# Longer first loads, narrower modulation products, fillers around c's turning, and a new engine order in a one-core transformer block

## The chip, the core and the metric

The kernel runs on one core of a Trainium2 chip. The core has five engines that run their own instruction streams and meet only at semaphores: TensorE (PE in the profile, with its weight loads shown as PEld), VectorE (DVE), ScalarE (ACT), GpSimd (POOL) and SyncE (SP), which only issues transfers. ScalarE issues transfers too. All transfers are carried by 16 DMA engines. The metric is the device time of one execution in microseconds (us), lower is better.

## The reference

The input `x` has 2048 rows of 448 columns. Two blocks follow each other, both conditioned on a vector `c`:

```
mod = (silu(c) @ w_mod), cut in six rows: sa, ca, ga, sb, cb, gb
h = layernorm(x) * (1 + ca) + sa
q, k, v = h @ wqkv, 16 heads of 28; causal attention over a window of 256
x = x + ga * (attention @ wo)
h = layernorm(x) * (1 + cb) + sb
z = gelu(h @ w_in);  z1 = z[:, :896];  z2 = layernorm(z[:, 896:])
g = w_sp @ z2 + b_sp                      (w_sp is 2048 x 2048)
x = x + gb * ((z1 * g) @ w_out)
```

Everything is bf16 in memory. The first modulation rows, sa and ca, are needed before any query or key can be made, so `c`, the first two rows' share of `w_mod`, and the q and k columns of `wqkv` are the first things that the kernel loads beside `x`.

## The kernel before

The rows of `x` are cut in 16 tiles of 128; four tiles make a block (`tb` 0 to 3), and the 448 columns are contracted in four chunks of 112 partitions. The work has four stages that overlap at their borders.

**Front.** Loads of `x` tiles 0 and 1, of `c`, of `w_mod` (tile `wmodA`) and of the q and k weights (tile `wq_st`) are issued from SP and ScalarE in turn. TensorE turns `c` into a column with four one-column products (L514), ScalarE applies silu and writes `sc_sb` (L517), and TensorE multiplies it with `wmodA` in 32 products (L544, `t_mA`), in four groups of eight, one per load. VectorE writes the result to `modT` (L573, L574). In the meantime `x` is normalised (statistics L626 and L629, reciprocal root on GpSimd L631 and L633, application L644 or L651), transposed by TensorE for block 0 (L740), and scaled by `modT` into `hT` (L749, L751). The weights are copied from `wq_st` into a padded tile `WQK` (L615, L616, eight copies). Then K (L821), Q (L797) and V (L841) of the first tiles are made. Products of a tile of ones, called fillers (L563, 36 of them), run on TensorE where it would have nothing to do.

**Attention.** Blocks 1 to 3 are transposed by DMA (L467) and scaled on any of three engines (L730, L732). For each of 16 tiles: scores (L926, L956, L967), exponentials on ScalarE (L912), masks on VectorE (L975, L996), products with V (L1003), reciprocal and scaling (L1017, L1019), turning by DMA, the output projection (L1029), the sum (L1033) and the second norm.

**z.** TensorE makes z2 and z1 (L1123, L1144), ScalarE applies gelu.

**Mixing.** 448 products with `w_sp` (L1168), 119 with `w_out` (L1187), and the stores.

**The order is written out.** `PLAN` is a string of words such as `p42.1` or `d108`. The letter names the engine (p TensorE, a ScalarE, d VectorE, t GpSimd, s SP), the number is the operation in the order in which the code creates it, and numbers behind dots choose a PSUM bank or buffer. Every engine runs its own words in the order of the string, and it waits at each for what the operation depends on; nothing behind a waiting word can pass it. Many operations can stand on two or three engines (helpers `free`, `either`, `lock_free`), so the letter is also the choice of engine. The string was searched by a planner that is not in the kernel. The numbers that calls such as `load4` and `pe` carry (landing times, durations) and the `after` lists served that planner; the program made from a given string does not use them, other than the dependencies.

Names that the steps use: `t_x0` (loads of x tiles 0 and 1, then 2 and 3), `t_wmA`, `t_wk` and `t_wq` (first loads, two by two on SP and ScalarE), `t_cT`, `t_sc`, `t_mA`, `t_modA`, `warm` (fillers), `wqk` (copies to `WQK`). The group of q, k and v products of the tiles is made in the loop over `tb` from L700 on.

Of the kernel before, what the change touches and what calls it, by code (L numbers as in the profile page):

```python
# [17 lines left out]
p145.6 p146 a147 p136.1 p137 a138 s11 p151.5 p152 a153 p79.2 t120 t121 d123.0 d122.1 p130.7 p133.0 a134 d41  # L18
d131 t184 t185 d186.3 p68.0 p372.0 a373.2 p142.6 p143 a144 d132 d135 p154.7 p170.1 p171 p155 p378.0 s13 d241
d247 d245 s14 d308 d242 d156 d246 s15 s193 t187 t188.1 s194 p163.0 p164 t189 t190.2 s195 t191 t192.0 s196  # L20
a379.4 p397.0 t34 t35 d248 t36 d243 d382 d312 d306 d380 d309 d374 d376 p173.6 a172 p157.1 p158 p160.7 p174
a398.1 a165 p90.0 p91 d92 a399 p404.0 d402 d310 d244 d400 d169 p161 p93.0 t85 t84 a175 a159 p86.1 p87 d88 d89
p375.0 p377 p94 a405.3 a406 p425.0 p381 p383 a197 d199 t200 d198 p210.1 p211 t249 t250 t252 t253.2 t254 d95
p217.0 p218 s16 s19 a426.0.0 p433.0 d384 d385.1 p401.0 s386 a166 d407 p403 p408 a212 p204.1 p205 d311 d219
p201.0 p202 d409 s259 t255.1 d307 d313 t314 d167 d168 s260 d251.0 t256 s258 t257.3 s261 t315 t321 t319 t99 t98
t96 t97 a434.2 p453.0 d429 d203 d436 a206 p207.1 p208 p410 d411 d209 d430 d412.2 s413 d435 a162 p427.0 p220.0
p221 a454.1.1 p461.0 p229.1 p230 d457 a428 a222 p226.0 p227 d228 p431.0 p432 a462.6 p481.0 d463 a231 a482.4.2
s852 s17 s18 p437 p438 d439 d215 d440.1 s441 p223.0 p224 a225 p232.1 d458 d216 d213 d464 p489.0 a490.2 d492
p233 p235.0 p236 a237 p459.0 p455.0 p508.0 p414.0 p415 d416 t262 t264 t263 t265 a234 p387.1 p388 d389 d486
a456 p460 p465 p466 d467 d468.0 d485 t320.1 s325 t322.2 s469 s326 s21 a214 p483.0 p272.0 p273 a509.0.0 p536.0  # L30
p269.1 p270 d491 p487.0 a484 p510.0 p488 p493 a537.5.1 p516.0 d274 d316.0 s323 t317 t318.3 p494 d390 d391 t392
t393 d512 d513 d495 d496.1 s497 d394.1 t395 s324 t330 t327 t329 a271 a511 p266.1 p267 p538.0 p275.0 p276
a517.6 d519 d518 d417 p564.0 a268 p442.1 a277 p282.0 p443 p514.0 d444 d281 p515 p283 a565.4.2 d569 p544.0 d418
d445 t419 d278 p291.1 p520 p521 d522 d446 d540 d447 d541 a539 p292 a284 p288.0 p289 t448 t449 s396 t450.0 t328
t451 s20 s848 d523.1 s524 a545.2 p572.0 d546 d547 d568 a293 p294.1 p295 a290 p238.0 p239 p542.0 p543 p548
# [217 lines left out]
def bass_adaLN_cond__sliding_block__mixer_gmlp__prompt_kernel(  # L253
# [13 lines left out]
    S, D, H, DH = 2048, 448, 16, 28  # L267
# [151 lines left out]
    for row in (t_x0[:1] + t_wmA[::2] + t_wk[:1] + t_x0[1:] + t_wq[:1], [t_c] + t_wmA[1::2] + t_wk[1:] + t_wq[1:]):  # L419
        for first, then in zip(row, row[1:]):  # L420
            then.after = [first]
# [147 lines left out]
    for op in fillers[30:]:  # L569
        op.deps.update(t_mA)  # L570
# [699 lines left out]
```

## Time and profile before

| | |
|---|---|
| three timed runs | 277.41, 279.69, 281.07 us; median 279.69 |
| the profiled execution, first to last instruction (span) | 276.2 us |
| distance of the median and of the fastest run from that span | 3.5 us and 1.2 us |
| TensorE busy | 269.2 us, 97% of the span |
| VectorE, ScalarE, GpSimd busy | 164.2, 124.1, 132.6 us |
| moved by DMA | 25.55 MB |

The span runs from the first to the last instruction of one profiled execution. The time of that execution as the runs are timed is not given apart; the three runs bound what lies around the span. A busy engine is one that has an instruction in flight. For TensorE that is not the same as running at full rate: the same product can follow its predecessor after a shorter or a longer time, and this is read from the start and the length of groups in the timeline. In rows of the timeline and of the chain the first number is the start in us from the span's start, the second the length in us.

### The profile page before, as it was taken

To read this page: it belongs to the slowest core of one execution; us is meant where nothing else is said; L and a number is where in the kernel's file an instruction comes from. 1 tells how busy PE (TensorE), PEld (TensorE's weight loads), DVE (VectorE), ACT (ScalarE), POOL (GpSimd) and SP (SyncE) were. 2 spreads that over 40 slices of the span, in tenths; PEclk is the share of its full clock that TensorE was granted. 3 is DMA by queue.
4 is the path that set the end of the run, shared out by engine and by line. 5 is a ranking of instruction groups with operands and counts; after the bars stand their busy time and mean duration, and the time that the engine had idled before them with its cause. 6 is when DMAs were issued, how large, how long until landed. Compare 5 with 4: busy or idle time off the path is not lost.

```text
span 276.2 us, 8438 instructions
## 1 busy us (share of the span) xinstructions
PE 269.2 (97%) x3751; PEld 155.0 (56%) x3751; DVE 164.2 (59%) x365; ACT 124.1 (45%) x146; POOL 132.6 (48%) x190
## 2 busy tenths in 40 slices
PE   7999999999999999999999999999999999999995
PEld 5976676687667766454444444444444444445452
DVE  3698999999998999968979310014302213121454
ACT  3399999998889888365885500000000000000000
POOL 7573899629185283667567003316643303241400
PEclk9999999999999999999999999999999999999999
DMA  7999548478152586768599996000000001000114
GB/s 197 267 299 188 88 80 194 89 84 133 41 60 42 44 136 148 127 115 134 108 172 188 152 220 118 0 1 0 2 0 0 17 2 33 0 0 2 33 50 133
DMA packets 67302, 25.55 MB, mean 92 GB/s; under 512 B 58497, under 2 KB 66178, under 8 KB 67266
## 3 DMA queue, kind: packets, MB, share of 16 engines
q1 hardware_dynamic: 66304, 24.21, 47.4%
q10 hardware_dynamic: 962, 0.80, 1.2%
q8 instruction: 29, 0.48, 0.8%
q14 instruction: 7, 0.06, 0.1%
HBM read 9.01 MB, written 1.84 MB: 39 GB/s over the span
## 4 chain that ended last, share of the span: by engine, by line
PE 83%; ACT 5%; DVE 4%; DMA 4%; POOL 2%; issue 1%; SPq 0%; DVEq 0%; POOLq 0%
PE ps L1168 35%; PE ps L1123 8%; PE ps L1144 8%; PE ps L1187 8%; PE ps L956 6%; PE ps L1003 5%; ACT PW L912 5%; PE ps L1029 4%; PE ps L763 4%; PE ps L821 3%; DMA hT<-xn 2%; PE ps L841 2%; DMA wmodA<-in_w_mod_dram 2%; DVE PT L975 1%; PE ps L544 1%; DVE st_all L626 1%
## 5 line engine op out<-in xcount | busy, mean ns | idle before, releaser
L1175 POOL TENSOR_TENSOR z1T<-tmpg,z1T 128x512 bf16<-128x512 bf16 x28 | 32.1, 1153 | 75.3 <-DVE tmpg L1172 75.3
L912 ACT ACTIVATE PW<-ps 128x2048 bf16<-128x2048 f32 (+1 forms) x42 | 59.8, 1450 | 7.5 <-PE ps L956 7.0
L1172 DVE TENSOR_TENSOR tmpg<-ps,bsp_bc 128x512 bf16<-128x512 f32 x28 | 19.0, 689 | 72.9 <-PE ps L1168 68.1
L1168 PE MATMUL ps<-wspB,z 128*128 128x512 bf16 x224 | 49.3, 379 | 0.0
L1168 PE MATMUL ps<-wspA,z 128*128 128x512 bf16 x224 | 49.0, 379 | 0.0
L975 DVE TENSOR_TENSOR PT<-PW,mask 128x1024 bf16<-128x1024 bf16 x56 | 41.6, 770 | 0.3
L1168 PEld LDWEIGHTS ps<-wspA,z 128*128 128x128 bf16 x224 | 21.9, 98 | 26.5 <-issue 0.4
L1168 PEld LDWEIGHTS ps<-wspB,z 128*128 128x128 bf16 x224 | 21.9, 98 | 26.3
L633 POOL TENSOR_TENSOR rs_all<-ve_all,neghalf 128x1 f32<-128x1 f32 (+2 forms) x37 | 25.1, 691 | 14.5 <-DVE ve_all L631 8.7
L1003 PE MATMUL ps<-Vaug,PT 128*128 128x32 bf16 x496 | 23.7, 177 | 0.3 <-issue 0.3
L1003 PEld LDWEIGHTS ps<-Vaug,PT 128*128 128x128 bf16 x496 | 21.5, 96 | 2.7 <-issue 0.8
L1123 PE MATMUL ps<-w_in,hT 64*128 64x448 bf16 x224 | 22.2, 349 | 0.1
L1144 PE MATMUL ps<-hT,w_in 64*128 64x512 bf16 x196 | 22.2, 376 | 0.0
L1187 PE MATMUL ps<-w_out_g,z1T 128*128 128x448 bf16 (+2 forms) x119 | 22.0, 342 | 0.0
L1197 DVE TENSOR_TENSOR fin<-ps,x_sb 128x448 bf16<-128x448 f32 (+2 forms) x17 | 9.7, 594 | 18.5 <-PE ps L1187 17.0
L626 DVE BATCH_NORM_STATS2 st_all<-x_sb 128x6 f32<-128x448 bf16 x32 | 18.9, 613 | 2.3 <-DMA x_sb<-in_A_x_dram 2.2
L1003 PE MATMUL ps<-Vaug,PW 128*128 128x32 bf16 x224 | 20.1, 176 | 0.0
L626 DVE BATCH_NORM_STATS2 st_all<-z 128x6 f32<-128x448 bf16 x32 | 18.7, 608 | 1.8 <-ACT z L1130 1.8
L651 POOL TENSOR_SCALAR xn<-x_sb,rs_all,ve_all 128x448 bf16<-128x448 bf16 x20 | 17.1, 858 | 4.8 <-DMA hT<-xn 3.5
L1152 ACT ACTIVATE z1T<-ps 128x512 bf16<-128x512 f32 x28 | 14.7, 601 | 9.2 <-PE ps L1144 9.1
L956 PEld LDWEIGHTS ps<-qT,KT 32*128 32x128 bf16 (+1 forms) x1344 | 13.5, 90 | 8.9 <-ACT PW L912 6.4
L1003 PEld LDWEIGHTS ps<-Vaug,PW 128*128 128x128 bf16 x224 | 17.6, 96 | 1.3
(103 smaller groups left out, 369.4 us busy)
## 6 DMA issues: line engine op xcount, KB each, us to landing
out_dram<-fin SPq DMA_DIRECT2D x15, 112.0 KB, 1.7
wmodB<-in_w_mod_dram SPq DMA_DIRECT2D x1, 1568.0 KB, 14.5
x_sb<-in_A_x_dram SPq DMA_DIRECT2D x3, 448.0 KB, 9.9
w_in<-in_B_w_in_dram SPq DMA_DIRECT2D x3, 448.0 KB, 5.9
w_out_g<-in_B_w_out_dram SPq DMA_DIRECT2D x1, 784.0 KB, 5.0
bsp_bc<-in_B_b_sp_dram SPq DMA_DIRECT2D x1, 512.0 KB, 5.7
x_sb<-in_A_x_dram SPq DMA_DIRECT2D x2, 224.0 KB, 4.9
hT<-xn SPq DMA_TRANSPOSE x28, 3.6
```

The source lines that it names most:

```text
L626: st = [dve(0.62 if True else 0, lambda e, t=t, ci=ci, s=s: e.bn_stats(st_all[:, slot, t, ci, :], s()), deps(t), prio) for ci, s in enumer ...
L633: return pool(0.4 + 0.15 * len(tiles), lambda e: e.tensor_tensor(rs_all[:, slot, a:b], ve_all[:, slot, a:b], neghalf[:, 0:b - a], ALU.pow) ...
L912: ex = act(xdur, lambda e, out_ap=out_ap, in_ap=in_ap: e.activation(out_ap(), in_ap(), ACT.Exp, scale=SCALE), [s] + list(after), v - 8.0 + ...
L956: fm.append(lambda e, hm=hm, qi=qi, key=key, kn=kn, lo=lo, hi=hi, col=col, p0=p0, t=t, j=j: e.matmul(ps[p0:p0 + kn, hm.slot[t], col:col + ...
L975: return lock_d(0.68, lambda e: e.tensor_tensor(cols(hp.slot[0] * 2048 + 1024 * k, [[256, 4], [128, 2], [1, 128]]), cols(at_w() + pad + at ...
L1003: fns.append(lambda e, hp=hp, hO=hO, hi=hi, bi=bi, kb=kb, hd=hd, nb=nb, a=at[hi][bi], p_of=p_of: e.matmul(ps[:, hO.slot[0], 32 * hd:32 * h ...
L1123: return lambda e, kc, p0, start, stop: e.matmul(ps[:, hs[t % 2].slot[hf], 0:D], lhsT=hT[p0:p0 + 64, kc, t * 128:(t + 1) * 128], rhs=w_in[ ...
L1144: return lambda e, kc, p0, start, stop: e.matmul(ps[:, hs[b // 2].slot[b % 2], :], lhsT=w_in[p0:p0 + 64, kc, ft * 128:(ft + 1) * 128], rhs ...
L1168: m = pe(16 * MMS, [lambda e, h=h, si=si, ft=ft, tb=tb: e.matmul(ps[:, h.slot[0], :], lhsT=z2[:, si, ft * 128:(ft + 1) * 128], rhs=(wspA i ...
L1172: a = dve(0.7, lambda e, h=h, ht=ht, tb=tb: e.tensor_tensor(tmpg[:, ht.slot[0], :], ps[:, h.slot[0], :], bsp_bc[:, tb * 512:(tb + 1) * 512 ...
L1175: u = pool(1.16, lambda e, ht=ht, ft=ft, tb=tb: e.tensor_tensor(z1T[tb][:, ft, :], tmpg[:, ht.slot[0], :], z1T[tb][:, ft, :], ALU.mult), [ ...
L1187: return [lambda e, ft=ft: e.matmul(ps[:, h.slot[0], 0:hi - lo], lhsT=z1T[t // 4][:, ft, (t % 4) * 128:(t % 4 + 1) * 128], rhs=w_out_g[:, ...
```

## The change

- The four loads of `wmodA` and the four of `wq_st` become two each. One load brings two of the four chunks with both halves side by side, so each row that a transfer copies has 1,792 bytes in place of 896. ScalarE issues the first two chunks, SP the last two. The bytes are the same. The eight copies to `WQK` now wait by chunk pair and not by q or k.
- The 32 products of `t_mA` have a moving side of 64 columns in place of 112, and their four groups go by chunk pair first.
- `t_cT` has a filler in front of each of its four one-column products, and holds a PSUM bank for them.
- 23 fillers in place of 36: eight ahead of `t_cT`, nine between it and `t_mA`, six behind.
- `PLAN` is another string. Operation numbers are lower by 4 from the loads on and lower by 17 behind the fillers, so `p139` of before is `p122` of after. The letters change too: 365 words of VectorE become 386, 186 of GpSimd become 161, 148 of ScalarE become 150 (two of its loads are gone), 398 of TensorE become 385 (13 fillers are gone).

```diff
-d24 d22 p50.3 p52.1 p55.0 p46.1 p57.0 p54.3 a0 a3 d23 p37.0 p71.0 p63.3 p69.1 p73.0 p74.1 p61.0 p62.3 p60.2 s1
-s2 d108 d110 s4 s6 s10 s8 s12 a5 a7 a9 a38 a39 p75.1 t27 t28 t29 t32 t33 t30 t31 a100 a106 d111 d109 t112 t113
-t26 p42.1 p43 p58.3 p48.1 p44.0 p45 d114.3 d115.1 p124.6 p77.2 p64.0 p51.3 d83 p127.0 p70.1 p66.0 p72.2 p67.3
-p65.0 p78.1 d82 d125 d128 t101 p139.1 t25 t102 p56.0 d126 p81.3 p76.1 p47.0 p80.3 p59.2 p53.1 p49.2 a105 t103
-d129 p140 a141 a40 p148.5 p149 a150 d116 d118 d117 d119 d176 d180 d182 d178 d177 d183 d181 d179 t104 t107
...
+d20 a0 s1 a2 t23 s3 d19 p42.0 s5 d91 p43.0 p44.0 p45.0 s6 p46.0 p47.0 p48.0 p49.0 p33.0.0 a4 a34 s8 d18 a35
+d93 t24 t25 t28 d94 d92 p50.0 p51.0 p52.0 t29 p53.0 t26 t27 d95 t96 d98.0 p54.0 p55.0 t21 t30 a88 t32 p56.0
+p57.0 p58.0 p38.0 p39.1 p40 p41 d97.1 p107.2 t83 d66 p110.3 d65 a111 a112 t84 p59.2 p60.2 p61.2 s7 d87 d108
+d109 d90 d89 d99 d101 d100 d102 d165 d159 d161 d163 d166 t103 a86 d160 p122.2 d162 p62.2 p63.2 p64.2 a85
+p119.3 p120 t104 d164 p123 p131.0 a121 a124 p132 d106.0 p355.0 d105.1 a133 p128.1 p129 d130 a356.0 t167 t168
...
-    t_wmA = [x for v in range(2) for x in load4("d_wmA%d" % v, wmodA, w_mod, slice(v * D, v * D + D), slice(v * D, v * D + D), -98.95, ((5.4, 4.9), (6.6, 6.3))[v])]
-    t_wk = load4("d_wk", wq_st, A_wqkv, slice(D, 2 * D), slice(D, 2 * D), -98.9, (8.4, 7.9))
-    t_wq = load4("d_wq", wq_st, A_wqkv, slice(0, D), slice(0, D), -98.8, (10.4, 9.3))
-    t_x0.append(load_x0(1, "sp", -98.85, 9.6))
+    t_wmA = load4("d_wmA", wmodA, w_mod, slice(0, 2 * D), slice(0, 2 * D), -98.95, (5.0, 5.5), ("act", "sp"))
+    t_wqk_st = load4("d_wqk", wq_st, A_wqkv, slice(0, 2 * D), slice(0, 2 * D), -98.9, (7.3, 7.8), ("act", "sp"))
+    t_x0.append(load_x0(1, "sp", -98.85, 8.6))
...
+    hCW = Hold(bL)
+    def busy(h):
+        return lambda e: e.matmul(
+            ps[:, h.slot[0], 0:256].rearrange("p (a b) -> p a b", b=128), lhsT=fill[:], rhs=fill[:].unsqueeze(1).broadcast_to([128, 2, 128]), start=True, stop=True)
-    t_cT = pe(0.46, [lambda e, ch=ch: e.matmul(
-        ps[0:CP, hC.slot[0], ch:ch + 1], lhsT=c_row[:, ch * CP:(ch + 1) * CP], rhs=one[:, 0:1], start=True, stop=True)
-        for ch in range(DC)], [t_c, t_p1], -91.0, [hC])
+    t_cT = pe(1.32, [fn for ch in range(DC) for fn in (busy(hCW), lambda e, ch=ch: e.matmul(
+        ps[0:CP, hC.slot[0], ch:ch + 1], lhsT=c_row[:, ch * CP:(ch + 1) * CP], rhs=one[:, 0:1], start=True, stop=True))],
+        [t_c, t_p1, t_fill], -91.0, [hC, hCW])
...
-        v, kp = n // 2, n % 2
+        kp, v = n // 2, n % 2
-            ps[0:CP, hA[v].slot[0], ch * CP:(ch + 1) * CP], lhsT=wmodA[0:CP, kc, v * D + ch * CP:v * D + (ch + 1) * CP],
-            rhs=sc_sb[0:CP, kc:kc + 1].broadcast_to([CP, CP]), start=(kc == 0 and ch == 0), stop=(kc == DC - 1 and ch == DC - 1))
+            ps[0:CP, hA[v].slot[0], 64 * ch:64 * ch + 64], lhsT=wmodA[0:CP, kc, v * D + ch * CP:v * D + (ch + 1) * CP],
+            rhs=sc_sb[0:CP, kc:kc + 1].broadcast_to([CP, 64]), start=(kc == 0 and ch == 0), stop=(kc == DC - 1 and ch == DC - 1))
-            [t_wmA[n], t_sc] + t_mA, -60.0, [] if kp else [hA[v]]))
+            [t_wmA[kp], t_sc] + t_mA, -60.0, [] if kp else [hA[v]]))
...
-    warm(30, 0.22, 900.0)
-    warm(6, 0.12, 901.0)
+    warm(17, 0.22, -99.0)
+    warm(6, 0.12, -59.0)
...
-    t_wqkk = [wqk(1, kc, t_wk[kc // 2], -56.0 + 0.1 * kc) for kc in range(DC)]
-    t_wqkq = [wqk(0, kc, t_wq[kc // 2], -55.0 + 0.1 * kc) for kc in range(DC)]
+    t_wqkk = [wqk(1, kc, t_wqk_st[kc // 2], -56.0 + 0.1 * kc) for kc in range(DC)]
+    t_wqkq = [wqk(0, kc, t_wqk_st[kc // 2], -55.0 + 0.1 * kc) for kc in range(DC)]
```

In the new string `a2` and `s3` are the loads of `wmodA`, `a4` and `s5` those of `wq_st`, `s6` is x tiles 2 and 3; `p33` is `t_cT`, `a34` the silu, `p38` to `p41` the products of `t_mA`, `p42` to `p64` the fillers; `d66` and `d65` write `modT`; `t83`, `t84`, `a86` and `a85` copy k's four chunks and `d87`, `a88`, `d89`, `d90` q's; `d108`, `a111`, `d109`, `a112` make `hT` of tiles 0 and 1; `p122` and `p123` make K of tile 0, `p119` and `p120` Q of tile 0; `d99` is the first statistic of tiles 2 and 3.

More of the change, by code (lines that the diff above doesn't have):

```diff
@@ L18 @@
[L18 to L32, printed above, removed]
@@ L77 @@
+p1146.0 p1086.2 d1087.3 s1088 d1147.1 s1148 s1183 p1149.7 d1150.0 s1151 d1144.3 p1189 s1145 p1152.6 d1153.1
+s1154 d1190.2 s1191 p1113.4 d1114.0 p1077.2 s1115 d1186.3 d1078.1 s1187 s1079
 """
@@ L856, in bass_adaLN_cond__sliding_block__mixer_gmlp__prompt_kernel @@
     for op in t_wv + t_x[1:] + t_wmB + t_wo:
-        op.after = t_wq[:1]
+        op.after = t_wqk_st[:1]
     for op in t_win_l:
```

122 lines of the change are left out of this document (68 added, 54 removed).

## The prediction

> **What bounds the kernel now.** I read the page first: busy times, slices, the chain by engine.
>
> ```profile
> span 276.2 us, 8438 instructions
> PE 269.2 (97%) x3751; PEld 155.0 (56%) x3751; DVE 164.2 (59%) x365; ACT 124.1 (45%) x146; POOL 132.6 (48%) x190
> PE   7999999999999999999999999999999999999995
> DVE  3698999999998999968979310014302213121454
> PE 83%; ACT 5%; DVE 4%; DMA 4%; POOL 2%; issue 1%; SPq 0%; DVEq 0%; POOLq 0%
> ```
>
> TensorE is the end's engine in 83% of the chain. Averages hide stages, so the windows by stage come next (columns: stretch, length, busy time of PE, PEld, DVE, ACT, POOL).
>
> ```profile
> 12.00:30.00 18.00, 17.47 (x314) 12.95 (x313) 16.52 (x48) 16.28 (x22) 10.30 (x19) 1.00 1.11 229
> 30.00:109.00 79.00, 77.49 (x2325) 56.62 (x2322) 74.95 (x149) 71.12 (x71) 50.02 (x66) 1.00 0.58 88
> 109.00:155.00 46.00, 45.95 (x471) 21.87 (x467) 39.66 (x109) 29.87 (x45) 29.54 (x56) 1.00 0.86 151
> 155.00:273.00 118.00, 118.00 (x569) 55.24 (x567) 27.77 (x44) 2.55 (x5) 35.02 (x31) 1.00 0.17 37
> ```
>
> From 109 to 273 TensorE has no gap and the products stay the same, so nothing is to be won or lost there: 164 us are fixed, and so is the tail of 3 us. From 30 to 109 three engines are near full together: VectorE is idle for 79.00 - 74.95 = 4.05 us, ScalarE for 7.88. What the edits in front win must pass through that stage. The front itself is read in the chain in order of time:
>
> ```profile
> 1.31 4.30 DMA wmodA<-in_w_mod_dram
> 5.75 1.72 PE ps L544 x16
> 7.46 0.43 PE ps L563 x2
> 7.89 1.49 PE ps L544 x16
> 9.38 0.33 PE ps L740 x4
> 10.30 1.05 DVE hT L751 x3
> 11.35 1.06 DVE st_all L626 x2
> 12.63 2.14 DVE st_all L626 x4
> ```
>
> So far a load, the modulation's products (3.2 us in two halves), the turning of xn, the scaling, then VectorE's statistics set the time.
>
> **The change, part by part.** *Products and fillers.* Both are priced by these rows of the timeline:
>
> ```profile
> 2.96 2.10 PE L563 MATMUL ps<-fill 128*128 128x256 bf16 x9
> 5.75 1.72 PE L544 MATMUL ps<-sc_sb,wmodA 112*112 112x112 bf16 x16 [0.68 <-DMA wmodA<-in_w_mod_dram]
> 11.26 1.04 PE L563 MATMUL ps<-fill 128*128 128x256 bf16 x8
> 25.70 0.54 PE L534 MATMUL ps<-sc_sb,wmodB 112*128 112x64 bf16 x12
> L563 PE MATMUL ps<-fill x36: 271/274/421, 1.1 to 16.6; 128*128 128x256 bf16 x36
> ```
>
> Nine fillers take 2.10 us early: less the last one's 0.42, eight steps of 0.21. Eight take 1.04 at 11.26: seven steps of 0.11. TensorE runs at half rate until some point before 11.26, although its granted clock is 1.00 in the windows. The modulation's 112 columns step by (1.72 - 0.30) / 15 = 0.095 us, slow; 64 columns late step by (0.54 - 0.19) / 11 = 0.032, fast, which at the slow rate is an estimated 0.054. The 32 products then cost 1.0 to 1.7 us in place of 3.2. The fillers of after run from 1.11 without a gap: eight slow ones to 2.8, `t_cT` with its four to about 4.1 (four times 0.21 and 0.10), nine to 6.0. The 0.68 us of idle time ahead of the first product goes only if the load is there by then.
>
> [...]
>
> *Loads.* The bytes, the queues and their order stay nearly the same. When they land is read from who waited:
>
> ```profile
> 8.55 0.58 ACT L616 ACTIVATE WQK<-wq_st 112x448 bf16<-112x448 bf16 x1 [2.71 <-DMA wq_st<-in_A_wqkv_dram]
> 9.98 0.58 ACT L616 ACTIVATE WQK<-wq_st 112x448 bf16<-112x448 bf16 x1 [0.85 <-DMA wq_st<-in_A_wqkv_dram]
> L406 SPq DMA_DIRECT2D wmodA<-in_w_mod_dram x2: 448/464/480, 1.3 to 1.8; - x2
> DMA to landing us min/median/max: 3.8/4.6/5.2
> ```
>
> The last of `wmodA` landed at 1.8 + 5.2 = 7.0, k's at 8.5, and ScalarE's queue had delivered its four loads (803 KB) when the copy at 9.98 could start. After, the same queue brings the same 803 KB in two loads, so at the same rate `a4` lands at 9.95, and k's first half lands later than before, not sooner. Whether rows of 1,792 bytes are faster stands in the rates of other rows (last column GB/s):
>
> ```profile
> 3.00:8.00 5.00, 4.32 (x32) 3.37 (x32) 2.11 (x6) 2.51 (x3) 2.64 (x6) 1.00 1.08 276
> 14.00:16.00 2.00, 2.00 (x30) 1.66 (x28) 1.97 (x9) 1.84 (x4) 0.79 (x2) 1.00 1.16 381
> 16.50:20.50 4.00, 3.99 (x66) 2.87 (x63) 3.94 (x10) 3.86 (x6) 3.59 (x8) 1.00 1.03 268
> ```
>
> From 3 to 8 it is these weights with 896 bytes; from 16.5 to 20.5 `wmodB`, the same tensor to the same 112 partitions with 3,584: 268, no better. From 14 to 16 mostly `x`, 128 partitions and 896 bytes: 381. So 268 and 381 are the bounds. The first speaks against any gain.
>
> [...]
>
> *What follows, at 276.* Modulation's last products end at about 7.0 + 0.1 + 0.5 to 0.9, near 7.8 in place of 9.4. But VectorE has `d87` (a copy that waits for `a4`) ahead of the scaling `d108`, and ScalarE `a88` ahead of `a111`; everything behind these two words waits for 9.95. These rows price it:
>
> ```profile
> 9.83 1.52 DVE L751 TENSOR_SCALAR hT<-ps,modT 112x256 bf16<-112x256 bf16 x4 [0.18 <-PE ps L740]
> 11.27 1.14 DVE L626 BATCH_NORM_STATS2 st_all<-x_sb 128x6 f32<-128x448 bf16 x2
> 12.14 1.51 PE L821 MATMUL ps<-hT,WQK 112*128 112x128 bf16 x24
> L846 DVE CAST Vaug<-ps 128x448 bf16<-128x448 f32 x2 | 1.2, 602 | 0.0
> L644 DVE TENSOR_SCALAR xn<-x_sb,mv_all,rs_all 128x448 bf16<-128x448 bf16 x4 | 1.6, 392 | 0.0
> L656 DVE COPY xn<-xn 128x64 bf16<-128x64 bf16 x1 | 0.2, 172 | 0.0
> L773 DVE CAST qT<-ps 128x512 bf16<-128x512 f32 x5 | 3.3, 665 | 0.3 <-PE ps L763 0.3
> L791 DVE COPY QBD<-qT 32x512 bf16<-32x512 bf16 x11 | 5.0, 458 | 0.3
> ```
>
> A copy to `WQK` on VectorE is not in the trace: between 0.17 (64 columns) and 0.60 (448 from PSUM); I take 0.39, as L644 has the same shape and memory. VectorE: 9.95 + three copies (1.17) + two scalings (0.4 each) = 11.9 for `d99`, against 11.27: 0.6 later. ScalarE: `a88`, `a111`, `a112`, `a86`, `a85` at 0.58 each end at 12.85. TensorE has Q of tile 0 (16 products of 128 columns, 0.06 each, 0.9 us) from 11.9 and the second half of K (0.5) from 12.9: done at 13.4. Before, the row at 12.14 has that half and K of tile 1 done at 13.5, as much work. So TensorE gains 0.1.
>
> At 381, the 6.9 us shrink to 5.0: `a4` at 8.1, `d99` at 10.1 (1.2 sooner), K at 11.0, after Q: 2.0 us ahead. TensorE's gain lies between 0.1 and 2.0. It is nearer the 268 row; I take 0.7, a third of the way. The 13 fillers fewer cost and win nothing by themselves: they stood where TensorE waited.
>
> *Order and engines.* GpSimd loses 25 words, VectorE gains 21. Compared operation by operation, VectorE gets five xn, three WQK copies and two wmodE copies (0.39 each), four V copies and one each of K, q and hT (0.60 each), 13 small ones (0.17); it gives up four q copies (0.665) and five QBD or hT pieces (0.46). Sum: 3.9 + 4.2 + 2.2 - 2.7 - 2.3 = 5.3 us. ScalarE has four instructions more, 2.3 us at 0.58. The ends for the attention stage are 0 (all in slack) and 5.3. Summing each engine's words with such means up to the last product with V, VectorE has only 0.5 us more than before and TensorE's work behind that point is equal; 4.05 us of idle cover 0.5, so I take 0. Uncovered, it costs 0.5. Of transfers, SP now issues `wmodB` ahead of x tiles 12 to 15: both are ahead of the turns of block 1 (L467) in either order, so these land with the same bytes before them: 0, at most the 0.6 by which VectorE is late.
>
> *Sum.* 276.2 - 0.7 + 0 = 275.5 for a profile. The runs lay 1.2 to 4.8 above the span, their median 3.5, so 279.69 - 0.7 = **279.0**. Their spread of 3.7 us is 1.3%; 2% (5.6 us) is about what a measurement of this kernel can tell from no change.
>
> **The rivals.** *Longer rows are faster:* 381 GB/s, the planner's landing times (7.3, 7.8) roughly hold, TensorE gains 2.0: 277.7. For it: 381 exists with 896-byte rows. Against it: 268 with 3,584.
>
> *VectorE becomes the bound (slower):* the moved 5.3 us fall in the front and in attention where VectorE is nearly full. Five of the copies (1.9) meet idle time in front; 3.4 stay, with the 0.6 of the late landing: 279.69 + 4.0 = 283.7. It decides once more than 4.05 us of new work or waits stand before the last mask; ahead of that mask the sums by words differ by 3.2, so it is close. Against it: up to the last product with V it is 0.5.
>
> *The new order closes attention's gaps:* half of VectorE's idle and the front's 2.0 are won: 279.69 - 4.0 = 275.7. Nothing in the trace says that a new string does so.
>
> *The edit does nothing of what it names:* the gap stays, since `wmodA`'s first half lands up to 7.0 and the fillers end at 6.0. That is inside the forecast; it costs the 0.4 us between fast and slow products.
>
> **How the numbers follow.** Forecast 0.50 (its own range 277.2 to 281.1, the runs' spread), faster rows 0.24, VectorE 0.18, closed gaps 0.08. Forecast and faster rows stay within 2% but for strays. Beyond 2% lie below 274.1 (closed gaps with all the idle won, 0.06) and above 285.3 (VectorE with 5.3 uncovered and 0.6 late, 285.6, or an order with new stalls, 0.11). Within: 0.83. The range holds forecast, faster rows and most of the two others: 275.0 to 283.7.
>
> **What would show it.** The copies of `wq_st` start near 9.95 (forecast) or 8.1. Fillers on either side of `t_mA` step by 0.21 or 0.11. The first L626 behind the copies starts near 11.5. VectorE's idle from 30 to 109 stays near 4 us; if it falls to 1 and the first L1168 starts later than 155.1, the slower rival holds. The prediction is wrong if the mixing stage or the tail changes length, which I hold fixed, or if new waits in attention reach several us.

## The result and the profile after

The changed kernel takes 292.04 us (median of four runs, 289.01 to 295.82) and the kernel before 279.39 (four runs): the ratio is 1.045, 95% interval 1.039 to 1.051. It is slower by 4.5%. The profiled execution has a span of 287.3 us and a time of 289.01, so 1.7 us lie around the span, and the span is 11.1 us longer than before.

The page of the changed kernel: the busy times, two engines and TensorE's granted clock in 40 slices, and the chain by engine.

```profile
span 287.3 us, 8410 instructions
PE 274.1 (95%) x3732; PEld 156.5 (54%) x3742; DVE 166.3 (58%) x386; ACT 126.8 (44%) x150; POOL 114.6 (40%) x165
PE   8999999989799998999999599999999999999996
PEclk9999999999999998899999989999999999999999
PE 73%; DVE 16%; DMA 6%; ACT 2%; issue 1%; SPq 1%; DVEq 0%
```

TensorE's share of the chain falls from 83% to 73%, VectorE's rises from 4% to 16%. There is a hole in TensorE's slices (the 5) at 160 us, just ahead of mixing, and the granted clock dips beside it and once before, between 108 and 122 us. The windows say in which stage the time goes (columns as in the prediction; the last three are granted clock, DMA share and GB/s):

```profile
30.00:109.00 79.00, 74.71 (x2196) 53.70 (x2196) 69.15 (x154) 71.00 (x74) 31.31 (x44) 1.00 0.60 89
109.00:155.00 46.00, 44.93 (x548) 22.50 (x546) 39.63 (x103) 30.28 (x40) 32.07 (x55) 0.96 0.86 138
155.00:165.00 10.00, 7.22 (x68) 3.11 (x66) 9.03 (x24) 6.19 (x12) 5.84 (x10) 0.98 1.07 194
165.00:170.00 5.00, 4.65 (x16) 2.00 (x18) 0.00 (x0) 0.00 (x0) 0.00 (x0) 0.70 0.91 179
```

VectorE did not become the bound of attention: from 30 to 109 it is busy 69.15 us and was 74.95. It idles more, and so does TensorE (74.71 against 77.49). The end of each stage is read from the first and last start of two groups, the reciprocals of the 16 tiles (attention's ends) and the products of mixing. Each pair of rows is the kernel before, then the changed one:

```profile
L1017 DVE RECIPROCAL rec_all<-ps x16: 241/253/258, 29.1 to 115.6; 128x16 f32<-128x16 f32 x16
L1168 PE MATMUL ps<-wspA,z x224: 379/379/390, 155.0 to 249.9; 128*128 128x512 bf16 x112
```

```profile
L1023 DVE RECIPROCAL rec_all<-ps x16: 235/258/258, 31.0 to 119.8; 128x16 f32<-128x16 f32 x16
L1174 PE MATMUL ps<-wspA,z x219: 379/379/634, 165.3 to 248.3; 128*128 128x512 bf16 x110
160.76 1.46 PE L1150 MATMUL ps<-hT,w_in 64*128 64x512 bf16 x12
165.35 1.91 PE L1174 MATMUL ps<-wspA,z 128*128 128x512 bf16 x4 [3.13 <-issue]
```

So the 11.1 us are: 1.9 until the first reciprocal (31.0 against 29.1), 2.3 in attention (88.8 against 86.5), 3.0 from there to TensorE's last product ahead of mixing (119.8 to 162.2, against 115.6 to 155.0), 3.1 of waiting, and 0.8 that mixing and the tail are longer, at the lower clock. From the last reciprocal to its last product TensorE has no wait, so the 3.0 are products that the kernel before had done by then; that fits with the 2.8 us that TensorE is less busy from 30 to 109.

A part of the 2.3 in attention is the first dip. The first row is its window in the changed kernel; the other two are the same 28 products of z there, and in f3, a run described below that has the same string and no such dip:

```profile
114.00:117.00 3.00, 3.00 (x16) 0.97 (x16) 3.00 (x6) 0.98 (x1) 2.90 (x6) 0.54 1.83 272
114.64 3.84 PE L1129 MATMUL ps<-w_in,hT 64*128 64x448 bf16 x28
```

```profile
113.80 2.82 PE L1129 MATMUL ps<-w_in,hT 64*128 64x448 bf16 x28
```

With the four products of a projection ahead of them (1.53 us for 0.92) TensorE is 1.6 us slower there. How much of it reaches the end isn't shown: from the first reciprocal to TensorE's last product f3 takes 131.7 us and the changed kernel 131.2. The front shows itself in the timeline:

```profile
1.11 2.23 PE L515 MATMUL ps<-fill 128*128 128x256 bf16 x9 [1.11 <-DVE one L485]
3.27 0.25 PE L518 MATMUL ps<-one,c_row 1*112 1x1 bf16 x1
3.78 0.25 PE L518 MATMUL ps<-one,c_row 1*112 1x1 bf16 x1
...
6.87 3.15 PE L549 MATMUL ps<-sc_sb,wmodA 112*112 112x64 bf16 x32
10.71 0.85 PE L515 MATMUL ps<-fill 128*128 128x256 bf16 x3
...
9.18 0.58 ACT L622 ACTIVATE WQK<-wq_st 112x448 bf16<-112x448 bf16 x1 [2.77 <-DMA wq_st<-in_A_wqkv_dram]
10.06 0.16 DVE L580 TENSOR_SCALAR modT<-ps 112x4 f32<-112x4 f32 x1 [3.11 <-PE ps L549]
11.75 1.14 DVE L632 BATCH_NORM_STATS2 st_all<-x_sb 128x6 f32<-128x448 bf16 x2
```

The 32 products take 3.15 us, a step of 0.093, and three fillers behind them still step by 0.21, the half rate. A one-column product and its filler take 0.51 us together (3.27 to 3.78), not 0.31.

### The profile page after: what moved, and what is told of

Same layout as the page of the kernel before. It is cut to its first block, busy times and chain, and to the rows that moved or that the text cites. A ratio compares the mean times of both kernels' runs of the same rounds, so it can differ in the third digit from the quotient of the medians.

```text
span 287.3 us, 8410 instructions
## 1 busy us (share of the span) xinstructions
PE 274.1 (95%) x3732; PEld 156.5 (54%) x3742; DVE 166.3 (58%) x386; ACT 126.8 (44%) x150; POOL 114.6 (40%) x165
## 4 chain that ended last, share of the span: by engine, by line
PE 73%; DVE 16%; DMA 6%; ACT 2%; issue 1%; SPq 1%; DVEq 0%
PE ps L1174 34%; PE ps L1193 7%; PE ps L1129 6%; DMA hT<-o_sb 5%; DVE st_all L632 4%; PE ps L1009 4%; PE ps L1150 3%; PE ps L827 3%; PE ps L1035 3%; DVE PT L981 3%; PE ps L962 2%; PE ps L847 2%; DVE z L1141 2%; PE ps L515 2%; PE ps L769 2%; DMA hT<-xn 2%
## 5 line engine op out<-in xcount | busy, mean ns | idle before, releaser
L1174 PE MATMUL ps<-wspA,z 128*128 128x512 bf16 x219 | 49.9, 386 | 3.3 <-issue 3.1
L981 DVE TENSOR_TENSOR PT<-PW,mask 128x1024 bf16<-128x1024 bf16 x56 | 37.9, 702 | 0.8 <-ACT PW L918 0.7
L639 POOL TENSOR_TENSOR rs_all<-ve_all,neghalf 128x1 f32<-128x1 f32 (+2 forms) x37 | 23.3, 640 | 15.7 <-DVE ve_all L637 7.7
L1009 PE MATMUL ps<-Vaug,PT 128*128 128x32 bf16 x496 | 23.1, 177 | 0.9 <-DVE xn L662 0.9
L1129 PE MATMUL ps<-w_in,hT 64*128 64x448 bf16 x224 | 23.0, 360 | 0.0
L657 POOL TENSOR_SCALAR xn<-x_sb,rs_all,ve_all 128x448 bf16<-128x448 bf16 x15 | 14.4, 962 | 16.1 <-DVE ve_all L655 14.1
L962 PE MATMUL ps<-qT,KT 32*128 32x128 bf16 (+5 forms) x1344 | 17.3, 197 | 1.4 <-ACT PW L918 0.8
L827 PE MATMUL ps<-hT,WQK 112*128 112x128 bf16 x256 | 17.6, 222 | 0.9 <-DVE qT L779 0.7
```

The source lines that it names most:

```text
L639: return pool(0.4 + 0.15 * len(tiles), lambda e: e.tensor_tensor(rs_all[:, slot, a:b], ve_all[:, slot, a:b], neghalf[:, 0:b - a], ALU.pow) ...
L827: km = lambda g, kc, start, stop, h=h, t=t: lambda e: e.matmul(ps[:, h.slot[0], g * 128:(g + 1) * 128], lhsT=WQK[0:CP, kc, 16 + 4 * g:20 + ...
L962: fm.append(lambda e, hm=hm, qi=qi, key=key, kn=kn, lo=lo, hi=hi, col=col, p0=p0, t=t, j=j: e.matmul(ps[p0:p0 + kn, hm.slot[t], col:col + ...
L981: return lock_d(0.68, lambda e: e.tensor_tensor(cols(hp.slot[0] * 2048 + 1024 * k, [[256, 4], [128, 2], [1, 128]]), cols(at_w() + pad + at ...
L1009: fns.append(lambda e, hp=hp, hO=hO, hi=hi, bi=bi, kb=kb, hd=hd, nb=nb, a=at[hi][bi], p_of=p_of: e.matmul(ps[:, hO.slot[0], 32 * hd:32 * h ...
L1129: return lambda e, kc, p0, start, stop: e.matmul(ps[:, hs[t % 2].slot[hf], 0:D], lhsT=hT[p0:p0 + 64, kc, t * 128:(t + 1) * 128], rhs=w_in[ ...
```

## The experiments

All ratios are to the kernel before, run on the same chip, with a 95% interval.

**The parts of the front.** Two edits alone in the kernel before:

```diff
-            rhs=sc_sb[0:CP, kc:kc + 1].broadcast_to([CP, CP]), ...
+            rhs=sc_sb[0:CP, kc:kc + 1].broadcast_to([CP, 64]), ...
```

> The kernel before with one edit: the modulation's 32 products have 64 columns in place of 112. The prediction took them at an estimated 0.054 us each at half rate; the changed kernel shows 0.093. Theory LOADBOUND (the weight load of 112 columns sets the step, so nothing gets faster): the two halves take about 1.7 and 1.5 us as before, 278.5 to 279.5 us. Theory RELEASE (products that stream less also hold back the full rate): the fillers behind them step by 0.21 in place of 0.11 and the time rises by 0.5 to 2 us. The prediction's own reading would give 1.5 us less in the front and up to 1.3 us less time.

Measured (f1): 278.57 us, ratio 1.001 (0.998 to 1.004). Nothing gets faster: 16 products of 64 columns took 1.67 us where 16 of 112 took 1.72. The step and the time are LOADBOUND's; that the weight load is the reason isn't shown, only that the streamed columns aren't it. In the profile the three fillers behind the products do take 0.85 us (0.49 before), as RELEASE has it, but the rise in time that it expects is not there: 0.5 us would be 1.002, inside the interval, 2 us would not.

```diff
-    t_wmA = [x for v in range(2) for x in load4("d_wmA%d" % v, wmodA, w_mod, slice(v * D, v * D + D), ...
+    t_wmA = load4("d_wmA", wmodA, w_mod, slice(0, 2 * D), slice(0, 2 * D), ...
```

> The kernel before with one edit: the first loads in rows of 1,792 bytes (four in place of eight), the fillers, products and the order else as before. If the bytes land 10 to 15% sooner, as in the changed kernel, and nothing waits for a first half that now comes with the second: 277.5 to 279 us. If k's first half, which came by itself at 8.5 us and now comes near 9.1, is what the front's statistics wait behind: 279 to 281 us. The prediction had 0 gain as its likeliest case.

Measured (f2): 278.93 us, ratio 1.002 (0.998 to 1.006). Longer rows are worth nothing in the sum, as forecast. In this front a loss can hide a gain: the first of the 32 products waits until 6.85 us (5.75 before), since its load now brings both halves.

**Front and order apart.** Each kernel takes the words of one string up to a point, and behind it the engines and the order of the other.

```diff
 t104 d164 p123
-p131.0 a121 a124 p132 d106.0 p355.0 d105.1 ...
+t22 a124 a36 p131.5 p132 a133 p128.6 ...
```

> The changed kernel's loads, products, turning and front, and behind the front (from the first attention word on) every operation on the engine and in the order of the kernel before. Theory FRONT (the front that ends late is passed on through attention to mixing): the time stays near the changed kernel's, 288 to 292 us, and mixing starts at 163 or later. Theory ORDER (the order searched anew costs, and attention takes up what the front is late): 279 to 283 us, and mixing starts by 158. In between, at 284 to 287, both would have their part: I hold FRONT at 0.35, ORDER at 0.45, both 0.2.

Measured (e1): 280.76 us, ratio 1.007 (1.003 to 1.011): ORDER by the time; mixing starts at 158.6, a little behind the 158 of that theory.

```diff
 d179 t104 t107
-p145.6 p146 a147 p136.1 p137 a138 s11 ...
+p79.2 p68.0 t34 t36 s11 t120 p136.3 p137 t121 ...
```

> The kernel before with its own loads, products, turning and front; behind the front every operation on the engine and in the order of the changed kernel. Theory ORDER: 287 to 292 us, the last z2 norm near 162 us and TensorE idle in front of mixing as in the changed kernel. Theory FRONT: 279 to 282 us, and mixing starts by 157. If both have their part, 283 to 287. With the run before it the two parts should add up to about 12.7 us, if they don't act on each other.

Measured (e2): 290.5 us, ratio 1.034 (1.023 to 1.045). TensorE waits 3.02 us in front of mixing, as ORDER has it. The two parts add up to 4.1%, of 4.5%. The order costs most, and the front, which I had at a gain, about 1.9 us. To find which edit of the front, one thing is undone in the run with the front alone, then in the changed kernel:

```diff
-            rhs=sc_sb[0:CP, kc:kc + 1].broadcast_to([CP, 64]), ...
+            rhs=sc_sb[0:CP, kc:kc + 1].broadcast_to([CP, CP]), ...
```

> The run with the changed kernel's front alone (280.8 us), with products of 112 columns in place of 64. Theory RATE (the products of 64 columns, each of them shorter than its weight load, keep TensorE from the full rate until they are over): the full rate comes sooner in most executions and the time is 278 to 279.5 us. Theory FRONT (c's turning with fillers in it, and the loads' and words' order, cost the 1.9 us): 280 to 281.5 us.

Measured (h1): 278.53 us, ratio 1.000 (0.997 to 1.002): RATE. The timelines of the run with 64 columns and of the run with 112:

```profile
6.73 3.15 PE L546 MATMUL ps<-sc_sb,wmodA 112*112 112x64 bf16 x32
10.57 0.85 PE L512 MATMUL ps<-fill 128*128 128x256 bf16 x3
```

```profile
6.89 3.12 PE L546 MATMUL ps<-sc_sb,wmodA 112*112 112x112 bf16 x32
10.30 0.49 PE L512 MATMUL ps<-fill 128*128 128x256 bf16 x3
```

The products last the same, but behind those of 112 columns three fillers take 0.49 us (full rate), behind those of 64 0.85. Of the 13 profiled kernels with this front and 64 columns, nine still had the half rate there; neither of the two with 112 had it. These counts alone would prove little: with the front of before and 112 columns, f2 has the half rate at 10.71 and e2 the full rate at 5.41. What speaks for RATE is the time, 1.000 against 1.007 with intervals that don't overlap.

> The changed kernel with modulation's products of 112 columns in place of 64, everything else as it is. Theory RATE: TensorE gets its full rate by 10 to 12 us in place of 13.5 to 16.6, and the time is 1 to 3 us less than the changed kernel's, 288 to 290.5 us; what is left against before is the order alone. If the lateness of the front is lost again in the later waits, 290.5 to 293 us.

Measured (f3): 289.27 us, ratio 1.036 (1.030 to 1.042), where the changed kernel has 1.045: the gain goes the way of RATE, but the two intervals overlap, so f3 by itself doesn't show it. Some 3.6% are left to the order.

**Local repairs of the order, by what the trace names.** VectorE holds 16% of the chain, so it is given less (33 words), and the turn for which it waits 2.0 us is issued sooner:

```diff
-d95
+t95
...
```

> The changed kernel with the 33 operations that the new order gave to VectorE, and that the kernel before had on GpSimd, given back to GpSimd at the same places of the order; nothing else is changed. Theory VECTOR (VectorE has too much work before the last z2 norm): it gets free of about 8 us, the last z2 norm ends at least 4 us earlier, mixing starts by 160 and the time is 284 to 287 us. Theory TURNS (VectorE waits for buffers that late DMA turns hold, and its work is no limit): at most 1.5 us are gained, 288 to 292 us.

Measured (e3): 290.03 us, ratio 1.042 (1.032 to 1.051). The window from 109 to 155, and two links of the chain:

```profile
109.00:155.00 46.00, 42.36 (x550) 21.83 (x550) 33.91 (x84) 29.51 (x39) 35.94 (x66) 1.00 0.79 132
```

```profile
136.50 1.65 POOL hT L1057 x2
...
164.22 1.36 DVE z L1138 x3
```

VectorE is busy 33.9 us there in place of 39.6, and still the last z2 norm ends at 165.6, later than the 164.2 of the changed kernel: between 104 and 141 us the chain now runs mostly over GpSimd and its DMA turns. VECTOR as I stated it falls.

```diff
-s241 p444.0 ...
+s369 s241 p444.0 ...
```

> The changed kernel with one edit: the DMA turn of tile 0's attention output is issued on SyncE ahead of a later tile's instead of at 43.2 us, so that its buffer comes free sooner. Theory TURNS: the waits of VectorE for an attention output buffer at 43 to 75 us (3.7, 3 and 2 us) get shorter by at least 2 us and mixing starts at least 2 us earlier, 286 to 289 us. Theory VECTOR: the waits move elsewhere and the time is within 1 us of the changed kernel's, 289 to 292 us.

Measured (e4): 287.86 us, ratio 1.032 (1.023 to 1.041). The median lies in the range of TURNS, but the profile has attention no sooner (119.8 in the changed kernel):

```profile
L1020 DVE RECIPROCAL rec_all<-ps x16: 234/258/258, 32.2 to 120.1; 128x16 f32<-128x16 f32 x16
```

The 3.7, 3 and 2 of the expectation are one row of the waits: the sum in us, the number and the longest. In e4 that sum is 3.8, the last z2 norm ends at 164.7, mixing starts at 165.1, and the interval overlaps with that of the changed kernel. TURNS is not shown.

**Halves of the order.** The cut is at the first products of z.

```diff
 d626 p704 t807
-p853.0 p854.1 s354 d755 ...
+t597 t598 s546 t515 ...
```

> The changed kernel up to the first products of z (its front and its order of the attention), and from there on every operation on the engine and in the order of the kernel before. The first runs leave some 8 to 10 us to the order searched anew; in the profiles the last reciprocal of the attention ends 1.1 us later than with the order of before (120.1 for 119.0 in the run with the front alone), the last z2 norm 6.8 us later (164.2 for 157.4). Theory Z (the new order of the z stage, which leaves VectorE's statistics and norms to the end, costs most of it): the last z2 norm ends by 160 and the time is 281 to 284 us. Theory ATTENTION (TensorE's waits for DMA turns between 30 and 110 push work behind 109): the z stage ends as late as before, 286 to 290 us.

```diff
 d600 p730.0 p775.0
-p853.0 p854.1 p855 p776 ...
+s833 s834 t624 t625 s832 d626 p853.0 ...
```

> The opposite half: the changed kernel's front, the order of before for the attention, and the changed kernel's order from the first products of z on. Theory Z: 285 to 289 us, VectorE's norms end at least 1.5 us behind TensorE's last product in front of mixing. Theory ATTENTION: 280 to 283 us, near the run with the front alone (280.8).

Measured: 293.31 us, ratio 1.052 (1.046 to 1.058) for g1, and 286.8, ratio 1.024 (1.016 to 1.031) for g2. The first tells nothing: at the seam the chain runs over GpSimd's norms, TensorE waits 6.15 us, and attention's last reciprocal ends at 127.9 (120.1). The second has attention as before and stands 1.7% above the front alone, nearly half of what the order costs: Z has its part. I first took the norms of the last four tiles, whose turns came late, for its cause:

```diff
-d705 p731 t597 ...
+d705 d706 d707 t708 t709 d710.0 d711 s712 p731 t597 ...
...
```

> The changed kernel with one thing moved: for the last four tiles (12 to 15) the words from the statistics of x1 to the DMA turn of the normed rows, and the four scalings behind them, stand right behind what they need, on the same engines. In the traces the turn of tile 12 is issued at 142.3 us though its x1 is there at 117.2; the last of these turns lands 24.6 us behind the attention's last reciprocal in the changed kernel and 19.4 to 19.6 with the order of before. Theory TAIL (these late norms hold back the last z products and with them VectorE's last z2 norms): the last turn lands by 140, the last z2 norm ends 3 to 5 us sooner, TensorE waits less than 1.5 us in front of mixing, 282 to 287 us. Theory LOAD (VectorE simply has too much to do there): the last z2 norm ends within 1.5 us of where it was, 288 to 292 us.

> The same move made in the run that has the front of the changed kernel, the attention's order of before and the z order of the changed kernel (286.8 us). Theory TAIL: 279 to 283.5 us, at most 2 us above the front alone (280.8). Theory LOAD: 285 to 288 us.

Measured: 305.33 us, ratio 1.087 (1.077 to 1.097) for g6, and 293.57, ratio 1.052 (1.046 to 1.058) for g9: far slower than either theory. The words stand "right behind what they need" in the string, so each engine stops at them until it is there, and everything behind them waits; in g6 TensorE's waits for the turns of attention's output rise to 8.3 us (2.4 in the changed kernel). TAIL is neither shown nor refuted.

**What TensorE waits for ahead of mixing.** The chain of the changed kernel in order of time (start, length) names VectorE up to 164.18, and then nothing for 1.17 us:

```profile
161.67 2.51 DVE z L1141 x4
164.18 1.17 issue
165.35 2.75 PE ps L1174 x6
```

If VectorE's queue is the cause, less work on z2 removes it:

```diff
-            rs = stats(2, [t], lambda t_: [lambda: z2[:, t_, 0:D], lambda: z2[:, t_, D:2 * D]], lambda t_, g=g: [g], v)
+            rs = stats(2, [t], lambda t_: [lambda: z2[:, t_, 0:112], lambda: z2[:, t_, D:D + 112]], lambda t_, g=g: [g], v)
-                z2[:, t, :], z2[:, t, :], mv_all[:, 2, t, 0:1], ...
+                z2[:, t, 0:D], z2[:, t, 0:D], mv_all[:, 2, t, 0:1], ...
```

> The changed kernel with VectorE's work on z2 cut: the statistics of a tile read 112 columns of each half in place of 448, and the norm writes 448 of 896 columns (the other half stays unnormed, so part of the normalisation of z2 is left out). That takes some 0.3 us from each of 32 statistics and 0.2 us from each of 16 norms. In the changed kernel the last norm ends 9.8 us behind the last gelu of z2 (6.2 before) and TensorE waits 3.1 us for it. Theory QUEUE (VectorE's queue of statistics and norms behind the last gelu costs this wait and the lower clock behind it): TensorE no longer waits in front of mixing, no lower clock there, 4 to 7 us less than the changed kernel, 284 to 288 us. Theory UPSTREAM (the z products themselves come late, because of the attention and the last tiles): 289 to 292 us. The rest of the loss, 5 us or more, stays in both cases if the gelus stay late.

> The same cut of VectorE's work on z2 in the kernel before (part of the normalisation of z2 is left out). There TensorE runs without a gap up to mixing and the last norm ends 1.1 us ahead of it. Both theories: the time stays within 0.7 us of the kernel before, so that what the cut brings in the changed kernel is a loss of its order and not work that every order pays for.

Measured: 287.9 us, ratio 1.028 (1.021 to 1.034) for k4, and for the same cut in the kernel before (k5) 278.58, ratio 1.000 (0.997 to 1.003). It helps only in the changed kernel, as QUEUE has it. But the norms now end at 158.4 and TensorE still waits, with no releaser named:

```profile
154.83 3.56 DVE L1141 TENSOR_SCALAR z<-z,mv_all,rs_all 128x448 bf16<-128x448 bf16 x9
163.62 4.65 PE L1174 MATMUL ps<-wspA,z 128*128 128x512 bf16 x13 [2.15 <-issue]
L465 SPq DMA_TRANSPOSE wspA<-in_B_w_sp_dram x16: 1168/1299/3651, 47.8 to 159.2; - x16
```

The third row gives the next suspect: the 16 turns of `wspA`, mixing's first weights, are issued on SyncE until 159.2. In the kernel before and in the changed one these turns, and SyncE's queue in the changed kernel:

```profile
L467 SPq DMA_TRANSPOSE wspA<-in_B_w_sp_dram x16: 1165/1302/1992, 39.7 to 145.6; - x16
```

```profile
L465 SPq DMA_TRANSPOSE wspA<-in_B_w_sp_dram x16: 1162/1301/3281, 48.8 to 161.2; - x16
144.88 7.68 SPq L465 DMA_TRANSPOSE wspB<-in_B_w_sp_dram  x5
...
153.23 4.48 SPq L465 DMA_TRANSPOSE wspA<-in_B_w_sp_dram  x2
157.76 1.31 SPq L465 DMA_TRANSPOSE wspB<-in_B_w_sp_dram  x1
159.11 3.37 SPq L465 DMA_TRANSPOSE wspA<-in_B_w_sp_dram  x2
```

The last is issued 16 us later than before, and between 144.88 and 159.11 six turns of `wspB` go ahead of it, whose first product starts at 204.4. Four words are moved on SyncE, in the changed kernel, in the one with the lighter z2, and in the run with attention's order of before with the lighter z2:

```diff
-s826 t880 ...
+s826 s821 s828 s824 s827 t880 ...
```

> The changed kernel with one edit on SyncE's queue: the last four turns of mixing's first weights (wspA) stand ahead of six turns of the second weights (wspB). In the changed kernel the last wspA turn is issued until 162.5 us and mixing starts at 165.35, 1.2 us behind the last z2 norm; in every run with the new z order whose landings the trace shows mixing starts 0.04 to 0.3 us behind the landing of the last wspA turn (160.3, 163.2, 163.5, 164.0), in the kernel before that turn is issued by 146.9. Theory WEIGHTS alone (SyncE's queue ends the wait in front of mixing, VectorE's norms are ready soon enough): TensorE's wait falls from 3.1 to under 1 us, 3 to 5 us less than the changed kernel, 285 to 289 us. Theory BOTH (the norms at 164.2 end it just as late): about 1 us less, wait about 2 us, 289 to 292 us.

> The same edit together with the lighter statistics and norms of z2 (part of the normalisation of z2 is left out, as in the run with the cut alone, 287.9 us). There the norms ended at 158.4, TensorE's products at 161.5, the last wspA turn landed at 163.5 and mixing started at 163.62. If the landing was what was left of the wait: mixing starts within 0.5 us of TensorE's last product, no lower clock behind it, 283 to 286 us. If the wait had another end (a buffer that the last gelus hold): within 1 us of the run with the cut alone.

> Both edits (turns of wspA ahead, lighter z2 statistics and norms, so part of the normalisation of z2 is left out) in the run with the changed kernel's front, the attention's order of before and the z order of the changed kernel (286.8 us). If the wait in front of mixing and the clock behind it are what the z order costs: 278.5 to 281.5 us, near the front alone (280.8), and the difference to the run with both edits in the changed kernel is the price of the attention's order, 3 to 5 us. If TensorE's own products come later by the z order: 282 to 285 us.

Measured: k7 287.29 us, ratio 1.027 (1.021 to 1.033); k6 286.83, ratio 1.030 (1.024 to 1.037); k8 282.33, ratio 1.013 (1.009 to 1.017). The start of mixing in the three:

```profile
162.11 8.15 PE L1171 MATMUL ps<-wspA,z 128*128 128x512 bf16 x37 [2.22 <-DVE z L1138]
```

```profile
160.98 9.23 PE L1171 MATMUL ps<-wspA,z 128*128 128x512 bf16 x42 [0.16 <-issue]
```

```profile
159.92 10.31 PE L1171 MATMUL ps<-wspA,z 128*128 128x512 bf16 x47 [0.16 <-issue]
```

With the weights early VectorE's norms are what is waited for (2.22 us, now named); with both edits the wait is gone. So the wait had two ends close together, and taking away either leaves some 2 us of it (3.13, 2.15, 2.22 and 0.16 us, each in one profiled execution). BOTH holds for the wait; the time of k7 lies in the range of WEIGHTS, but in its profile the shorter wait is the smaller part of the gain. Stage by stage k7's profile is 4.5 us shorter than the changed kernel's: 0.8 until the first reciprocal, 1.8 in attention and 1.3 from the start of mixing on (in these two stages the changed kernel has its two dips of the clock and k7 none), and 0.9 of waiting; 0.3 are lost in between. The edit comes too late in the string to reach the first two. k6 missed its 283 to 286: its profiled execution has a span of 281.6 us, but its median is not below that of k7. k8 is 0.6% above the front alone (280.8), 1 us more than expected; TensorE has two waits of 1.6 and 0.6 us left in its z stage.

**What attention's order costs.** In k6 TensorE's waits from 30 to 109 are led by the output projections, which wait for DMA turns (3.2 us). Three of them are put later, the first also in another PSUM bank:

```diff
-p575.0 p481.1 p482 d377.0 ...
+p575.0 d377.0 ... p583.0 p481.0 p482 ...
...
```

> The run with both edits in front of mixing (286.83 us, part of the normalisation of z2 is left out), and on top of it the output projections of tiles 4, 5 and 6 three to seven words later on TensorE, their sums with x just behind. In that run TensorE waited at these projections 0.52, 0.29 and 1.59 us for the DMA turn of the attention's output. Theory PROJECTION (these waits are what the new order of the attention costs): the three waits fall below 0.5 us in sum, the last reciprocal of the attention ends at least 1.5 us sooner than 118.2 and mixing starts by 159.5, 282 to 285 us. Theory SLACK (the order is late for other reasons, and TensorE's idle only moves): TensorE's waits from 30 to 109 stay above 4 us, the last reciprocal stays within 1 us, 285 to 288 us.

Measured (k9): 288.14 us, ratio 1.037 (1.032 to 1.042). TensorE's waits from 30 to 109, before the edit and after it:

```profile
PE ps L1032 <- DMA hT<-o_sb: 3.2, 4, 1.6
PE ps L824 <- DVE qT L776: 1.1, 1, 1.1
PE ps L959 <- ACT PW L915: 0.6, 3, 0.2
```

```profile
PE ps L1006 <- DVE o_sb L1022: 2.1, 2, 1.9
PE ps L1006 <- DVE PT L978: 0.9, 1, 0.9
PE ps L1032 <- ACT qT L775: 0.9, 1, 0.9
PE ps L824 <- DVE qT L776: 0.7, 1, 0.7
```

The turns are waited for no more, but VectorE and ScalarE are, for 5.9 us with the shorter waits (4.9 before): TensorE's idle moves, as SLACK has it. But the last reciprocal ends at 121.9, 3.7 us later, of which 1.7 come from the front, where SLACK allowed 1 us, and the time is just above its range. Moving these projections brings nothing; whether their waits cost anything in the order as it was, and what attention's order costs otherwise, is left open.

## Why the prediction was wrong

It said 279.0 us and 275.0 to 283.7; 292.04 is outside, on the side to which it gave 0.11. Put one behind the other, the runs with their ratios (times 279) price the parts: the front with 112 columns 0.0 us (1.000), the 64 columns 2.0 (1.007), the z order without its wait 1.8 (1.013), attention's order 4.8 (1.030), the wait ahead of mixing with the lower clock behind it 4.0 (1.045); each with an interval of about 1 to 2.5 us on either side.

The border between the last two is the least sure, since it rests on the five executions of k6: 283.35 and 284.27 us at a granted clock of 1.00, and 286.83, 288.29 and 288.46 at 0.988 to 0.994. All five of k8 have 0.999 or 1.00 and take 281.40 to 282.97. At full clock, then, attention's order costs 1.5 us (283.81 against 282.33, from two executions of k6). The profiles agree with the smaller price: from the first to the last reciprocal it is 1.2 us more in k6 than in k8, 2.3 more in the changed kernel than before (with the dip of the clock), and 0.8 less in e2, which has the new order of attention behind the front of before. The rest stands in executions with a lower clock. That the clock is its reason is argued and not shown: in f3 and k9 the executions at 1.00 are not the shortest.

- **"164 us are fixed, nothing is to be won or lost there."** This step failed: of the 11.1 us of span 6.9 stand in the stretch that it held fixed, 3.1 of waiting ahead of mixing, 0.8 behind it, and 3.0 up to TensorE's last product before it, of which attention may be the source. The products are the same, but the step took TensorE's gapless run up to mixing in the old trace for a property of the work. It was one of the old order: `wspA` was issued by 146.9 us, and the norms ended 1.1 us ahead of mixing. In the changed kernel the last turn of `wspA` is issued until 162.5 and the norms end at 164.2; with both brought forward (k6) the wait falls from 3.13 to 0.16 us. The queue of SyncE was weighed only for the front, with `wmodB` and the turns of block 1. Every word on a queue moves when the whole string is new, and those that feed the longest stage had to be looked up one by one. I named a mixing stage that changes length as what would make the prediction wrong, and it did.
- **"I take 0" for order and engines.** The moved 5.3 us were summed by engine and compared with idle time. The sum was harmless: VectorE has more idle time in attention than before, and giving 33 words back (e3) brought nothing clear of the noise. TensorE loses 2.8 us from 30 to 109 with no engine fuller than before, so the cost is in who waits for whom, which no sum of busy times shows; which waits cost it stays open (k9).
- **The slower rival, VectorE as the bound.** Its place was wrong. It was set before the last mask; VectorE idles more there. Where it did delay TensorE was behind the last gelu, with 9.8 us of statistics and norms left where there had been 6.2.
- **"0.054 each"** for the 64-column products. This was mis-sized: 0.093 at half rate, as before. I scaled the step with the columns; the row that seemed to bear it out (L534, 0.032) has weights of another form, 128 columns (`112*128`) in place of 112. f1 shows that the moving columns are not what sets the step, and the full rate says the same: 0.052 with 64 columns (k4, its last 12 products in 0.79 us) and with 112 (e2, 16 in 1.00 us). Whether the weight load sets the step isn't shown; no run changes it alone.
- **When the full rate comes.** I left open whether the 32 products run at the slow or the fast step (0.5 to 0.9 us behind the load) and held both to lie inside the forecast. The profiled changed kernel has the full rate only at about 14 us (the fillers at 12.53 still step by 0.21, and 24 products with `WQK` from 14.63 take 1.50 us), k4 with the same front by 9.1 (three fillers in 0.49 us). The times of h1 and e1 say that the narrow products cost 2.0 us, and the sum had nothing on this.
- **Fillers "without a gap", ending at 6.0.** The pairs of c's turning take 0.51 in place of 0.31, and the fillers end at 7.07; the products start behind them, at 6.87, and the trace shows no wait for the load there.
- **Loads: no gain.** Right in the time (f2). The bytes did come sooner than at the lower bound: the copies of `wq_st` start at 9.18, between 8.1 and 9.95. The first statistic, at 11.75 for 11.9, is right by luck: the prediction had VectorE wait for the load of `wq_st` until 9.95, but it waited 3.11 us for the products of the modulation, which end at 10.0 and not at 7.8, and its three copies then took 0.7 us and not 1.17.
- **TensorE 0.7 sooner behind the front.** Wrong in sign with 64 columns, and with 112 the front is worth nothing that can be measured (1.000).

## What to carry to other kernels

When an order is exchanged as a whole, list for the longest stage what it needs (each weight turn, each norm) and where the new order issues it; a gapless engine in the old trace says nothing of the new one. A wait that the profile puts down to one engine can have a second end just behind it: remove one cause, and see whether the wait moves or goes. Moving words by hand in a searched order mostly moved the wait here (e4, g6, g9, k9), since every engine stops at the first word that isn't ready. And read the granted clock stage by stage before a difference of 1 or 2 us is put down to an edit.

## What the runs showed of the hardware

- **The step of narrow products.** A product with 112 columns of weights steps by 0.093 to 0.095 us at half rate (32 in 3.15 us in the changed kernel; 16 of 64 streamed columns in 1.67 us in f1 and 16 of 112 in 1.72 in the kernel before) and by 0.052 at full rate (64 columns in k4, 112 in e2). In the new front the narrow ones cost 0.7% (e1 against h1), and the full rate came late more often behind them: it was missing behind the products in nine of 13 profiled kernels with 64 columns and in neither of two with 112. What decides when it comes can't be told from these runs. In the kernel before, whose products begin sooner (at 5.75 us, in the changed kernel at 6.87) and in two halves, the narrow ones cost nothing measurable (f1, 1.001).
- **The clock can drop behind a short wait, and in these runs the length of the wait doesn't decide it.** In front of mixing the profiled kernels have these waits of TensorE: behind 3.13 us (changed kernel), 2.15 (k4) and 3.81 (g2) the granted clock of a window of 5 us fell to 0.70, 0.73 and 0.66, and behind 2.25 (f3) and 3.03 (e3) its mean from 165 to 205 us was 0.97 and 0.96; behind 2.22 (k7), 2.30 (e4) and 3.02 (e2) that mean was 1.00. The changed kernel's first dip (0.67 from 113 to 114 us, 0.50 to 116, 0.62 to 117, then 1.00) follows a wait of 0.87 us that ended at 111.98. From its start on, mixing with the tail takes 121.95 us in the changed kernel and 120.7 in k7, e4 and e2, so the drop costs an estimated 1.3 us, the difference of the two.

```profile
165.00:170.00 5.00, 5.00 (x18) 2.04 (x17) 0.00 (x0) 0.00 (x0) 0.00 (x0) 0.73 0.92 187
```

```profile
162.00:167.00 5.00, 4.89 (x23) 2.25 (x23) 0.00 (x0) 0.49 (x2) 0.00 (x0) 1.00 0.85 179
```

```profile
163.00:168.00 5.00, 4.47 (x21) 2.18 (x23) 0.00 (x0) 0.11 (x1) 0.00 (x0) 1.00 1.00 202
```

The three rows are windows behind the start of mixing: in the run with the lighter z2 (k4), in the one with the weights first (k7) and in the one with the new order alone (e2).
